# The second block's root ahead of the loop, its solve dealt sooner, and some small products moved, in a delta-rule attention with two MLPs behind it

## The chip, the cores and the metric

One core of a Trainium2 chip runs the whole program. The metric is the device time in microseconds (us) of one execution, as the median of timed runs. The engines are TensorE (PE in the rows; PEld is its loading of weights), VectorE (DVE), ScalarE (ACT), GpSimd (POOL) and SyncE (SP), which issues most DMAs. Each engine works through its instructions in the order in which the program has them and waits where an operand is not ready.

## The reference

Three stages, all in float32. The first is a recurrent attention with a delta rule, for 4 batches of 8 heads, 768 tokens, head size 48:

```
k_n = k / (norm(k) + 1e-6)
for t in range(768):
    y[t]  = q[t] @ state
    v_old = state^T @ k_n[t]
    state = state + beta[t] * outer(k_n[t], v[t] - v_old)
```

The second mixes its output by Fourier transforms over tokens and features, normalizes, and adds an MLP (384 to 1536 to 384). The third is a gated MLP whose gate is a product over tokens (768 x 768). The change touches only the first.

## The kernel before

**Chunks and steps.** The 768 tokens of a head are cut into 12 chunks of 64. The loop runs over 48 chunks (4 batches of 12, numbered `bc`, the batches staggered), each with all 8 heads of its batch. Within a chunk the recurrence is a triangular system of 64 x 64, and its inverse is put together from two 32 x 32 triangles that are inverted on VectorE and a product between them. Eight chunks make a block: block 0 is chunks 0 to 7, and there are 6 blocks.

**What a chunk passes through.** `stage_a(bc)` multiplies keys by keys and by queries on TensorE (16 matmuls as the trace counts them below chunk 24, 8 above) and copies the results to a tile `gak` on ScalarE. `prep(blk)` on VectorE gathers the triangles of 8 chunks and transposes them (L254, L261), and takes their diagonal, the squared norms (L263). `root(blk)` takes their square root on ScalarE (L141) and has GpSimd clear some triangles (L146). `solve(blk)` is the inversion on VectorE: scaling (L153 on), some 30 rounds of multiply and add (L308, L313), and two transposes into the tile `Tc` (L327). For blocks 1 to 4 `prep` of the next block, and then its `root`, stand inside `solve`, ahead of and between these last two transposes; `solve` does not go on to this `prep` while `stage_a` has not been issued for the chunks of the next block. `merge(g8, ...)` joins the two triangles of a pair of chunks by small products (32 each, 64 where it does a first and a second half), `diag` copies from `Tc` on ScalarE, and `stage_b`, `stage_c`, `stage_d` apply the inverse and update the state; `stage_c` ends in a subtraction on VectorE (L495) for which `stage_d` of the same chunk waits.

**The first block.** It is solved ahead of the loop in another form, `halves(0)`: VectorE inverts four 16 x 16 triangles instead of two of 32, and TensorE joins them by small products, `right(q)` (64 matmuls) and `left(q)` (72) for each pair of chunks `q`, each with a copy on ScalarE behind it. `left(q)` needs the copy of `right(q)`. `busy(1, 512)` is two matmuls of 512 columns whose result nobody reads. Keys and queries of chunks 0 to 7 are multiplied by `pairs0`, and for the queries ScalarE copies the result (L583).

**The loop** runs over steps t = -3 to 47. Step t has `stage_d(t)`, `stage_c(t + 1)`, `stage_b(t + 2)`, in odd steps a `merge` for the pair after, and `stage_a` some 20 chunks ahead. A step with t mod 8 = 5 starts a new block: at t = -3 for block 0, and at t = 5 the first merge that uses block 1's `Tc`. The solve of the next block is dealt out between: `Spread(gen, total)` advances `solve` until the sum of the costs that it yields (in ns) has reached a share of `total`, here (i + f) / 8, with i the step within the block and f = 0.5, 0.65 and 1 at three places of a step. Before, steps up to 4 issue one `stage_a` each and step 4 two (chunks 23 and 24), and the root of block 1 stands at the end of step -3.

**What fixes the order.** `chain()` ties each instruction of an engine to the one before it, so each engine's order is the program's. DMAs are issued on SyncE's queue in program order as well, with `load_kq` the keys and queries of a chunk (448 KB), `load_kv` keys and values (192 KB).

Of the kernel before, what the change touches and what calls it, by code (L numbers as in the profile page):

```python
# [23 lines left out]
NBC = B * NC  # L24
BLK = 8
NB = NBC // BLK
# [4 lines left out]
HEAD = 24  # L31
# [13 lines left out]
CF = dict(  # L45
    skew=4, ring=20, kq=5, qt=3, mb=2, cvd=3, cve=2, kn=4, sv="hhhhhd", few=3,
    warm=8, keep=1, last=1, cuts=(0.5, 0.65), dfs=(1, 1, 1, 1, 2, 2, 3, 1, 2, 2, 3, 0), cvt=(0, 0, 0, 1, 2, 2, 1, 1, 0, 0, 0, 0), early=5, first=8, ahead=3,
    turns=(4, 6, 7, 9, 10, 12, 13, 15, 16, 16, 17, 17, 18, 18, 19, 20), stats=(((0, 1, 2, 3, 3), (2,)), ((21, 22, 22), (23, 24, 25))),
)
# [17 lines left out]
class Kernel:  # L67
# [36 lines left out]
    def load(self, out, in_):  # L104
        return self.nc.sync.dma_start(out=out, in_=in_)
# [13 lines left out]
    def attention(self, cp, pg, pe, p, x, filler, after_solves):  # L119
        nc, a, load = self.nc, self.a, self.load  # L120
# [16 lines left out]
        def root(blk):  # L137

            Tf, T, Tw, sq = preps[blk]
            n0 = pe.tile([128, 32], F32, name="n0", bufs=2)  # L140
            nc.scalar.sqrt(n0, sq)  # L141
            if blk:

                for n in (16, 8, 4, 2, 1):
                    t = Tw[:, n : n + 1056].rearrange("p (m q) -> p m q", q=66 * n)[:, :, : 32 * n]
                    nc.gpsimd.memset(t.rearrange("p m (r w) -> p m r w", w=32)[:, :, :, :n], 0.0)  # L146
            preps[blk] = Tf, T, sq, n0
# [33 lines left out]
        def pairs0(n, i):  # L181

            pa = self.bank("pa", [128, 2 * HP, C])
            for g in range(2 * HP):
                k, y = (gas[m][i // 2][:, i % 2 * 2 + g // HP, g % HP] for m in "k" + n)
                for r, q in ROWS:
                    nc.tensor.matmul(pa[q, g], lhsT=k[r], rhs=y[r], start=True, stop=True)
            return pa

        def both0(i, at):  # L190
            return gas[i // 2 * 4, 4][:, i % 2 * 2 : i % 2 * 2 + 2, :, at : at + C].rearrange("p a b c -> p (a b) c")
# [10 lines left out]
        def load_kq(bc):  # L202
            if bc < HEAD:
                if 8 <= bc and bc % 2 == 0:
                    t = pe.tile([112, HP, 4 * C], F32, name="kq", bufs=CF["kq"]).rearrange("p a n -> p (a n)")
                    kqs[bc], kqs[bc + 1] = (t[:, i * HP * 2 * C : (i + 1) * HP * 2 * C].rearrange("p (a n) -> p a n", a=HP) for i in range(2))
                    load(out=t.rearrange("p (c n) -> p c n", c=2), in_=a["kc"][:, bc - 8 : bc - 6])
            elif bc < NBC:
                kqs[bc] = pe.tile([112, HP, 4 * C], F32, name="kq", bufs=CF["kq"])
                load(out=kqs[bc], in_=a["kq"][bc])  # L210

        def stage_a(bc):
            kq = kqs.pop(bc)
            if bc % 4 == 0:
                ring(bc)
            pa = self.bank("pa", [128, HP, 2 * C])
            for hp in range(HP):
                if bc < HEAD:
                    for r, q in ROWS:
                        nc.tensor.matmul(pa[q, hp], lhsT=kq[r, hp, C:], rhs=kq[r, hp], start=True, stop=True)  # L220
                else:
                    nc.tensor.matmul(pa[:, hp], lhsT=kq[:, hp, 2 * C :], rhs=kq[:, hp, : 2 * C], start=True, stop=True)  # L222
            if bc < HEAD:

                copy_g(gas[bc][:, :, C : 2 * C], pa[:, :, C:])
                nc.scalar.copy(out=gas[bc][:, :, :C], in_=pa[:, :, :C])
            else:
                copy_g(gas[bc][:, :, C : 2 * C], pa[:, :, C:])
                nc.vector.tensor_tensor(out=gas[bc][:, :, :C], in0=pa[:, :, :C], in1=mask_a(bc, C).to_broadcast([128, HP, C]), op=MUL)
            if bc < HEAD:  # L230
                if bc % 2 and bc + 2 * CF["kq"] < HEAD:
                    load_kq(bc + 2 * CF["kq"] - 1)
            else:
                load_kq(bc + CF["kq"])
            seen_a[0] = bc + 1
# [301 lines left out]
        for n in "kq":  # L537
            t = p.tile([128, 4, HP, GA], F32, name="gak", bufs=3).rearrange("p a b c -> p (a b c)")[:112, :2048]
# [25 lines left out]
        def busy(n, cols):  # L564
            wb = self.bank("pd", [128, cols])
            for i in range(n):
                nc.tensor.matmul(wb, lhsT=warm[:, :128], rhs=warm[:, :cols], start=True, stop=True)
# [9 lines left out]
                next(first)  # L577
        for _ in first:
            pass
        root(0)  # L580
        right, left = halves(0)
        for i in range(4):
            nc.scalar.copy(out=both0(i, 0), in_=pairs0("q", i))  # L583
        for bc in range(8, 16):
            stage_a(bc)
        busy(CF["last"], 512)
        for part, q in ((right, 0), (right, 1), (left, 0), (left, 1)):
            part(q)
        mask_q(0)
        for _ in prep(1):  # L590
            pass

        self.chain()

# [2 lines left out]
        solver, c1, c2 = None, *CF["cuts"]  # L597
        R = CF["ring"]
        T0 = -3

        lead = {-3: HEAD, -2: HEAD + 1, 0: HEAD + 2, 2: HEAD + 3, 4: HEAD + 4}
        rest = {-3: ((right, 2), (right, 3)), -2: ((left, 2),), -1: ((left, 3),)}
        for t in range(T0, NBC):
            j, i = divmod(t + 11, 8)
            if i == 0 and j < NB:
                if solver:
                    solver.finish()
                solver = Spread(solve(j), 28600 if j < NB - 1 else 27800)
            deal = lambda f: solver.upto((i + f) / 8)

            part = deal if T0 < t and j < NB else (lambda f: None)
            if light(t) and solver:
                solver.finish()
                solver = None

            if 0 <= t + 2 < NBC and (not light(t) or (t + 2) % 8 == 0):
                values(t + 2)
            if t % 2 == 0 and 2 <= t + 2 < HEAD:
                mask_q(t + 2)
            part(c1)  # L620
            if t >= 0:
                stage_d(t)
                if SEQ[t][1] == NC - 1:
                    fill.extend(filler(SEQ[t][0]))
            new = t % 8 == 5 and t + 3 < NBC
            if new:

                merge((t + 3) // 2, True, False)
                load_kv(t + 3)
                load_kv(t + 4)  # L630
                diag((t + 3) // 2)
            if 0 <= t + 1 < NBC:
                stage_c(t + 1)
            if light(t + 1) and t + 3 < NBC and (t + 3) % 8:
                values(t + 3)
            part(c2)
            if t + R <= HEAD:
                stage_a(t + R - 1)
                if t in lead:
                    load_kq(lead[t])  # L640
            if HEAD <= t + R < NBC:
                stage_a(t + R)
            for half, q in rest.get(t, ()):
                half(q)
            odd = t % 2 and (t + 3) // 2 < NBC // 2
            if t == NBC - 12:
                solver.finish()
                loads, tail = after_solves()
            if t % 2 == 0 and t % 8 != 4 and t + 4 < NBC:
                diag((t + 4) // 2)  # L650
            if (odd or light(t + 1)) and 0 <= t + 2 < NBC:
                stage_b(t + 2)
            if odd:
                g = (t + 3) // 2
                merge(g + 1, (g + 1) % 4 > 0, True)
                if (t + 5) % 8 and t + 5 < NBC:
                    load_kv(t + 5)
                    load_kv(t + 6)
            if light(t + 1):

                for _ in range(CF["dfs"][t - (NBC - 12)]):
                    while fill and next(fill[0], 1) == 1:
                        fill.pop(0)
                for _ in range(CF["cvt"][t - (NBC - 12)]):
                    next(tail, None)
            elif not odd and 0 <= t + 2 < NBC:
                stage_b(t + 2)
            if 2 <= t + 4 < NBC:
                load_qt(t + 4)
            if t == T0:  # L670
                root(1)
                part = deal
            part(1)
            self.chain()
            next(loads, None)
            if t >= NBC // 2:
                next(self.words, None)
            self.chain()
# [757 lines left out]
```

## Time and profile before

| | |
|---|---|
| timed runs, median (lowest to highest) | 869.68 us (868.71 to 870.67) |
| the profiled execution | 866.29 us, its span 864.5 us |
| mean granted TensorE clock | 0.978 |
| PE busy | 811.7 us (94%), 10509 matmuls |
| PEld busy | 772.6 us (89%) |
| DVE busy | 606.2 us (70%) |
| ACT busy | 419.8 us (49%) |

The span is the time from the first to the last instruction; the execution's own time is 1.8 us more. TensorE is busy in most of it, so a place where it is idle, or runs at the lower of its two clocks, is looked for. Times in the rows below are us from the start of the span. A matmul of float32 shows as two records, so a product of 32 small matmuls shows as x64. "issue" marks time in which an engine waited for nothing that the profile shows.

### The profile page before, as it was taken

How to read it: one execution, taken by the hardware profiler on the slowest of the kernel's cores; microseconds unless marked ns; L12 is line 12 of the kernel's file. 1: busy time of each engine (PE TensorE's matmuls, PEld its weight loads, DVE VectorE, ACT ScalarE, POOL GpSimd, SP SyncE). 2: the span in 40 equal slices, each digit the busy share in tenths (PEclk: the TensorE clock that was granted, in tenths of full speed). 3: DMA queues.
4: the chain of work that ended last, by engine and by line, in shares of the span. 5: the costliest groups of instructions: out<-in, count | busy, mean ns of one | idle time of the engine just before them, and what ended most of it. 6: DMA issues, size and time to landing. Idle time of an engine off the chain costs nothing.

```text
span 864.5 us, 25181 instructions
## 1 busy us (share of the span) xinstructions
PE 811.7 (94%) x10509; PEld 772.6 (89%) x10509; DVE 606.2 (70%) x1797; ACT 419.8 (49%) x1070; POOL 6.3 (1%) x40
## 2 busy tenths in 40 slices
PE   7696999897888899999999999999999999999998
PEld 7686887786778799989999999999999999899998
DVE  6396999898977898675463793436688378476563
ACT  3476878896756644233223362223471362553632
POOL 0000000000000000000000000000000000000000
PEclk9778999999999999999999999999999999999999
DMA  9344666555461600001022411112101201101101
GB/s 229 112 114 127 168 180 185 166 165 150 129 173 49 235 4 1 2 0 29 1 59 83 134 28 28 29 43 67 46 1 39 72 5 49 59 18 42 52 1 55
DMA packets 57955, 67.63 MB, mean 78 GB/s; under 512 B 31857, under 2 KB 48978, under 8 KB 57842
## 3 DMA queue, kind: packets, MB, share of 16 engines
q1 hardware_dynamic: 57698, 65.89, 26.4%
q8 instruction: 82, 1.34, 0.6%
q14 instruction: 31, 0.25, 0.1%
q10 hardware_dynamic: 144, 0.15, 0.1%
HBM read 53.62 MB, written 4.72 MB: 67 GB/s over the span
## 4 chain that ended last, share of the span: by engine, by line
PE 79%; DVE 9%; ACT 7%; issue 4%; DMA 1%; SPq 0%; ACTq 0%; DVEq 0%
PE bankX L917 17%; PE bankY L930 15%; PE bankX L1115 10%; PE bankX L1095 6%; PE bankX L1063 6%; PE bankY L1143 5%; PE bankY L494 3%; PE bankY L479 2%; PE bankZ L449 2%; PE bankX L222 2%; PE bankV L930 2%; PE bankX L730 2%; PE bankY L514 1%; PE bankY L513 1%; PE bankX L220 1%
## 5 line engine op out<-in xcount | busy, mean ns | idle before, releaser
L930 PE MATMUL bankY<-w,hx 128*128 128x384 f32 x756 | 147.2, 336 | 0.0
L917 PE MATMUL bankX<-uh,w 128*128 128x384 f32 x504 | 137.7, 340 | 0.7 <-DVE ul L839 0.7
L930 PEld LDWEIGHTS bankY<-w,hx 128*128 128x128 f32 x756 | 132.4, 188 | 0.5 <-issue 0.3
L922 DVE SCALAR_TENSOR_TENSOR hx<-bankX,hx 128x384 fp32r<-128x384 f32 x84 | 46.1, 549 | 75.8 <-ACT hx L921 73.3
L921 ACT ACTIVATE hx<-bankX 128x384 fp32r<-128x384 f32 x84 | 41.2, 490 | 112.3 <-PE bankX L917 107.6
L917 PEld LDWEIGHTS bankX<-uh,w 128*128 128x128 f32 x504 | 92.1, 188 | 1.2 <-DVE ul L839 0.9
L1115 PE MATMUL bankX<-w,A 128*128 128x384 f32 x504 | 88.8, 334 | 0.0
L1115 PEld LDWEIGHTS bankX<-w,A 128*128 128x128 f32 x504 | 87.6, 188 | 0.0
L917 PE MATMUL bankX<-ul,w 128*128 128x384 f32 x252 | 85.1, 338 | 0.0
L494 PE MATMUL bankY<-gak,WU 64*64 64x112 f32 x704 | 45.7, 266 | 10.5 <-issue 6.4
L514 PE MATMUL bankY<-WU,gak 64*64 64x48 f32 x768 | 49.5, 222 | 1.4 <-ACT x L531 1.4
L1095 PE MATMUL bankX<-xh,s 128*128 128x384 f32 x192 | 50.0, 338 | 0.0
L313 DVE TENSOR_TENSOR Ts<-Ts,tm 128x108 f32<-128x108 f32 (+10 forms) x216 | 48.8, 261 | 0.9
L308 DVE TENSOR_TENSOR tm<-Ts 128x108 f32<-128x108 f32 (+10 forms) x216 | 48.5, 260 | 0.4
L1104 ACT CAST u<-hx 128x384 fp32r<-128x384 f32 x32 | 15.8, 514 | 66.7 <-DVE hx L1102 66.7
L494 PEld LDWEIGHTS bankY<-gak,WU 64*64 64x64 f32 x704 | 35.9, 137 | 13.1 <-issue 7.4
L917 PEld LDWEIGHTS bankX<-ul,w 128*128 128x128 f32 x252 | 47.3, 188 | 0.0
L479 PE MATMUL bankY<-gak,TT 64*64 64x96 f32 x768 | 45.0, 258 | 1.5 <-ACT n L141 1.3
L514 PE MATMUL bankY<-Sb,cw 48*64 48x48 f32 x704 | 44.9, 220 | 1.4 <-DVE cw L495 1.4
L513 PE MATMUL bankY<-Sb,cw 48*48 48x48 f32 x640 | 37.1, 206 | 9.8 <-DVE cw L495 7.4
L1063 PE MATMUL bankX<-s,xh 128*128 128x512 f32 x144 | 45.9, 395 | 0.0
L513 PE MATMUL bankY<-WU,gak 64*64 64x48 f32 x704 | 43.5, 220 | 0.9 <-issue 0.8
(238 smaller groups left out, 1830.8 us busy)
## 6 DMA issues: line engine op xcount, KB each, us to landing
kq<-in_kq_dram SPq DMA_DIRECT2D x24, 448.0 KB, 4.0
qt<-in_qt_dram SPq DMA_DIRECT2D x48, 196.0 KB, 3.9
gak<-in_kv_dram SPq DMA_DIRECT2D x48, 192.0 KB, 4.1
w<-in_w_dram SPq DMA_DIRECT2D x24, 384.0 KB, 6.5
out_dram<-x SPq DMA_DIRECT2D x24, 192.0 KB, 1.9
kq<-in_kc_dram SPq DMA_DIRECT2D x8, 448.0 KB, 9.8
x<-x SPq DMA_DIRECT2D x96, 36.0 KB, 1.9
s<-in_wi_dram SPq DMA_DIRECT2D x6, 512.0 KB, 4.3
```

Of the source, the lines that this page charges most:

```text
L308: nc.vector.tensor_tensor(out=tm, in0=T[:, r, k : k + 1].to_broadcast(sh), in1=T[:, k : k + 1, :k].to_broadcast(sh), op=MUL)
L313: nc.vector.tensor_add(o, o, tm)
L479: nc.tensor.matmul(pb[h, hp].rearrange("p t d -> p (t d)"), lhsT=tt[h, o + hp], rhs=kv[h, hp], start=True, stop=True)
L494: nc.tensor.matmul(pc[h, hp], lhsT=w[h, hp, :C], rhs=gas[bc][h, hp, : C + D], start=True, stop=True)
L513: nc.tensor.matmul(ps[C * i : C * i + n - C, hp], lhsT=k[:, C:n], rhs=u, start=not last, stop=end)
L514: nc.tensor.matmul(po[hs[1 - i], hp], lhsT=k[:, :C], rhs=u, start=not last, stop=end)
L917: nc.tensor.matmul(ph, lhsT=w1[f][i][:, c * 128 : c * 128 + 128], rhs=cur[k][:, c], start=(c + j == 0), stop=(c == 2 and j == 2))
L922: nc.vector.scalar_tensor_tensor(out=hl, in0=ph, scalar=0.0, in1=hh.bitcast(F32), op0=MAX, op1=SUB)
L930: nc.tensor.matmul(acc[t], lhsT=hx[i][:, t * 128 : t * 128 + 128], rhs=w2[e][k], start=(e == 0 and j == 0), stop=(e == 11 and j == 2),)
L1063: nc.tensor.matmul(pv, lhsT=xT[t][i][:, c, kk * 128 : kk * 128 + 128], rhs=wi[2 * c + 1][k], start=(c + j == 0), stop=(c == 2 and j == 2))
L1095: nc.tensor.matmul(pu, lhsT=wi[2 * c][i][:, f * 128 : f * 128 + 128], rhs=xT[hf][k][:, c], start=(c + j == 0), stop=(c == 2 and j == 2))
L1115: nc.tensor.matmul(acc, lhsT=A[:, m, o, i, kk], rhs=Bo[name, kk][:, k], start=(kk + j == 0), stop=(kk == 2 and j == 2))
```

## The change

Ahead of the loop: three of the four query copies stand ahead of `root(0)`; two more `stage_a` (16, 17) and then a third (18) come in; `busy` goes; `root(1)` comes to the end of this part. In the loop: `stage_a` runs two chunks further ahead up to step 1 (19 in step -3 to 23 in step 1), with none in steps 2 and 3; the loads of chunks 24 to 26 are issued together in step -3, 27 in step -1, 28 in step 1. `right` and `left` of the third pair stand at the end of step -2, `right(3)` at the end of step -1 and `left(3)` at that of step 0. The solve of block 1 is dealt from the beginning of step -3, as if it had a total of 34000 instead of 28600.

```diff
@@ -577,18 +577,21 @@
                 next(first)
         for _ in first:
             pass
+        for i in range(3):
+            nc.scalar.copy(out=both0(i, 0), in_=pairs0("q", i))
         root(0)
         right, left = halves(0)
-        for i in range(4):
-            nc.scalar.copy(out=both0(i, 0), in_=pairs0("q", i))
-        for bc in range(8, 16):
+        nc.scalar.copy(out=both0(3, 0), in_=pairs0("q", 3))
+        for bc in range(8, 18):
             stage_a(bc)
-        busy(CF["last"], 512)
-        for part, q in ((right, 0), (right, 1), (left, 0), (left, 1)):
-            part(q)
+        for half, q in ((right, 0), (right, 1), (left, 0)):
+            half(q)
+        stage_a(18)
+        left(1)
         mask_q(0)
         for _ in prep(1):
             pass
+        root(1)
 
         self.chain()
 
@@ -598,17 +601,15 @@
         R = CF["ring"]
         T0 = -3
 
-        lead = {-3: HEAD, -2: HEAD + 1, 0: HEAD + 2, 2: HEAD + 3, 4: HEAD + 4}
-        rest = {-3: ((right, 2), (right, 3)), -2: ((left, 2),), -1: ((left, 3),)}
+        lead = {-3: (HEAD, HEAD + 1, HEAD + 2), -1: (HEAD + 3,), 1: (HEAD + 4,)}
         for t in range(T0, NBC):
             j, i = divmod(t + 11, 8)
             if i == 0 and j < NB:
                 if solver:
                     solver.finish()
-                solver = Spread(solve(j), 28600 if j < NB - 1 else 27800)
+                solver = Spread(solve(j), 34000 if j == 1 else 28600 if j < NB - 1 else 27800)
             deal = lambda f: solver.upto((i + f) / 8)
-
-            part = deal if T0 < t and j < NB else (lambda f: None)
+            part = deal if j < NB else (lambda f: None)
             if light(t) and solver:
                 solver.finish()
                 solver = None
@@ -634,14 +635,10 @@
             if light(t + 1) and t + 3 < NBC and (t + 3) % 8:
                 values(t + 3)
             part(c2)
-            if t + R <= HEAD:
-                stage_a(t + R - 1)
-                if t in lead:
-                    load_kq(lead[t])
-            if HEAD <= t + R < NBC:
-                stage_a(t + R)
-            for half, q in rest.get(t, ()):
-                half(q)
+            if t + R + 2 < HEAD or HEAD <= t + R < NBC:
+                stage_a(t + R + 2 * (t < 4))
+            for bc in lead.get(t, ()):
+                load_kq(bc)
             odd = t % 2 and (t + 3) // 2 < NBC // 2
             if t == NBC - 12:
                 solver.finish()
@@ -667,9 +664,13 @@
                 stage_b(t + 2)
             if 2 <= t + 4 < NBC:
                 load_qt(t + 4)
-            if t == T0:
-                root(1)
-                part = deal
+            if t == -2:
+                right(2)
+                left(2)
+            if t == -1:
+                right(3)
+            if t == 0:
+                left(3)
             part(1)
             self.chain()
             next(loads, None)
```

## Rows read from the trace of the kernel before

**Rows 1.** The page's part 2: tenths in 40 slices of 21.6 us.
```profile
DVE  6396999898977898675463793436688378476563
...
PEclk9778999999999999999999999999999999999999
```

**Rows 2.** The chain that ended last, 76 to 82 us: start, length, what.
```profile
76.71 1.33 DVE Cc L254 x2
...
78.07 1.91 DVE Ts L261
...
80.19 2.00 DVE Tc L327 x2
```

**Rows 3.** Timeline of PE: opening, step 0, stall at step 5, products at both clocks.
```profile
15.11 2.52 PE L187 MATMUL bankX<-gak 48*64 48x64 f32 x49 [2.29 <-issue]
...
25.35 1.12 PE L567 MATMUL bankY<-TT 128*128 128x512 f32 x2
...
26.41 0.79 PE L393 MATMUL bankY<-Tc,gak 32*32 32x16 f32 x72
...
46.62 1.92 PE L220 MATMUL bankX<-kq 48*64 48x128 f32 x16
...
53.21 0.25 PE L513 MATMUL bankY<-WU,gak 64*64 64x48 f32 x1
...
68.38 0.98 PE L494 MATMUL bankY<-gak,WU 64*64 64x112 f32 x16 [0.56 <-ACT WU L481]
...
69.19 1.04 PE L220 MATMUL bankX<-kq 48*64 48x128 f32 x16
...
82.25 1.06 PE L447 MATMUL bankZ<-Tc,gak 32*32 32x32 f32 x32 [6.14 <-DVE w L153]
...
83.24 1.76 PE L494 MATMUL bankY<-gak,WU 64*64 64x112 f32 x16
```

**Rows 4.** Timeline of DVE: start, length, operation; in brackets idle before, releaser.
```profile
43.98 0.18 DVE L153 TENSOR_SCALAR w<-n 128x32 f32<-128x32 f32 x1 [13.96 <-ACT n L141]
...
66.13 0.60 DVE L495 TENSOR_TENSOR cw<-qt,bankY 112x448 f32<-112x448 f32 x1
...
76.29 0.42 DVE L229 TENSOR_TENSOR gak<-bankX,mk 128x256 f32<-128x256 f32 x1 [5.66 <-ACT gak L196]
```

**Rows 5.** Timeline of DVE in the opening.
```profile
24.99 1.01 DVE L382 STREAM_TRANSPOSE V<-Ts 128x512 f32<-128x512 f32 x1
...
29.83 0.19 DVE L263 COPY sq<-Ts 128x32 f32<-128x32 f32 x1
```

**Rows 6.** The chain that ended last, 36 to 44 us.
```profile
36.90 3.44 issue
...
43.72 0.24 ACT n L141
```

**Rows 7.** The page's parts 3 and 6: the instruction queue; one key load.
```profile
q8 instruction: 82, 1.34, 0.6%
...
kq<-in_kq_dram SPq DMA_DIRECT2D x24, 448.0 KB, 4.0
```

**Rows 8.** Windows: length; busy us (count) of five engines; clock, DMA share, GB/s.
```profile
15.10:22.30 7.20, 7.19 (x125) 7.19 (x127) 7.20 (x60) 3.89 (x13) 0.93 (x3) 0.76 1.01 234
...
30.90:34.90 4.00, 3.29 (x128) 2.81 (x128) 0.00 (x0) 2.24 (x7) 0.00 (x0) 0.72 0.23 56
...
34.90:40.30 5.40, 1.94 (x128) 1.70 (x128) 0.00 (x0) 0.73 (x2) 0.00 (x0) 0.50 0.48 124
...
82.20:88.90 6.70, 6.65 (x136) 5.90 (x136) 4.35 (x18) 2.21 (x7) 0.15 (x1) 0.62 0.39 97
```

**Rows 9.** Timeline of ACT in the opening.
```profile
13.04 0.23 ACT L141 ACTIVATE n<-sq 128x32 f32<-128x32 f32 x1 [7.63 <-DVE sq L263]
...
16.07 0.58 ACT L583 COPY gak<-bankX 128x512 f32<-128x512 f32 x1 [1.84 <-PE bankX L187]
...
31.98 0.27 ACT L404 COPY Tc<-bankY 128x128 f32<-128x128 f32 x1 [2.59 <-PE bankY L403]
```

## The prediction

> **What bounds the kernel now.** I read the page's slices first. VectorE is busy for 7 to 9 tenths of nearly every slice up to 280 us, but for 3 tenths of the second (21.6 to 43.2 us) and 6 of the fourth, and TensorE's granted clock is 7, 7 and 8 tenths in the second to the fourth [rows 1]. So the opening has two holes, and the change lies in the opening.
>
> Next, the chain of waits in the fourth slice. At step 5 the matrix of block 1 (Tc, 8 chunks solved at once) is first used by a merge on TensorE. The chain there is VectorE alone: prep(2) in two adds (L254), its transpose (L261) and the two transposes of Tc (L327), which end at 82.2 [rows 2]. TensorE stood idle for 6.14 us before that merge [rows 3]. VectorE's timeline shows why it was late: after 66.13 it had only tails of solve(1) and two small jobs left, and then sat idle 5.66 us until the evictions of step 4 [rows 4]. In the code this is `while seen_a[0] < 8 * blk + 16`: prep(2) stands inside solve(1), ahead of the transposes, and stage_a(23) comes only in step 4.
>
> The other hole: VectorE waits 13.96 us for the root of block 1 [rows 4]. That root is one ScalarE instruction (L141, 0.23 us), ready from the end of prep(1) at 30.0 [rows 5]; but it is written at the end of step -3, behind a merge that TensorE ends only after a 3.44 us stop, and starts at 43.72 [rows 6].
>
> The stops without a releaser are the last thing to see. TensorE's 10509 + 10509 instructions in 82 packets are 256 a packet, 16 KB each [rows 7]. Between stops the trace counts exactly 128 matmuls with their 128 weight loads: 30.9 to 34.9 and 34.9 to 40.3 are two such stretches, 4.0 and 5.4 us long, with 3.3 and 1.9 us of work in them [rows 8]. So small products are limited by instruction fetch, one packet at a time, and the longer stretch is the one with the busier DMA (0.48 against 0.23). With DMA full, at 1.01, the packet begun at 15.1 lasted TensorE 7.2 us [rows 8].
>
> The Trainium skill, "Runtime: NRT & Kernel Launch", Instruction fetch mechanics, has the same 256-instruction blocks, but calls the cost of crossing one "mostly hidden". By that rule the 2.29 us stop in the query products [rows 3] would not return and the first root would lose 0.4 us rather than 3.5; the forecast below would be nearer 855. The rows here contradict it, and I follow the rows.
>
> **The change, part by part.** Times are of the profiled execution, 866.29 us with its 864.5 us span; the three timed runs have a median of 869.68, so I take differences and subtract them from the median.
>
> *Query copies ahead of the first root: a loss.* Order on ScalarE is program order. The root now starts at 13.04; the copy of the third query product waits for TensorE until 16.07 and takes 0.58 [rows 9], because that product is cut by the 2.29 us fetch stop before 15.11 [rows 3]. TensorE's instructions up to there are unchanged, so the stop stays. The root moves to about 16.6, +3.5 us, and VectorE, which has no idle time from there on, moves with it: Tc of block 0 from 25.0 to 28.5, V from 26.0 to 29.5, the end of prep(1) from 30.0 to 33.5 [rows 5]. Bounds: 0 if the stop falls elsewhere, 3.6 if not. I take 3.5.
>
> *Two more stage_a (16, 17) ahead of the products, the two 512-column warm-up matmuls out.* These matmuls took 1.12 us [rows 3] while TensorE waited for VectorE. The two stage_a cost 1.04 each at full clock and fill the same wait, now 3.5 us longer. Nothing either way.
>
> *Second root ahead of the loop: the gain's source.* It comes behind the copy of left(1). Before, right(0) to that copy ran from 26.41 to 31.98 [rows 3, 9], 5.6 us with two fetch stops in it. Now it starts at 28.5 and carries stage_a(18) too, 1.0 to 1.9 us: 35.5. Bounds: 33.7 (prep(1) ends) to 39 (one more slow fetch). So solve(1) starts at 35.7 rather than 43.98, 8.3 us earlier.
>
> *Solve dealt over 34,000 rather than 28,600, from the start of step -3.* Summing the yields of solve(1) gives 28,100 with prep(2), 22,500 without. Before, VectorE needed 22.15 us from 43.98 to 66.13 [rows 4] for what the plan counts as 5.5/8 of 28,600 = 19.7, two masks and one or two query subtractions, so the plan's units are real time. After, 5.5/8 of 34,000 = 23.4 stand there, 3.7 more: this subtraction comes at 35.7 + 22.2 + 3.7 = 61.6 in place of 66.1. The rest of the solve is 4.7 us: Tc is ready by 66.4, the next subtraction at 67. prep(2) needs stage_a(23), which now lies in step 1, so the 5.66 us idle goes. Root 2 goes into step 3 with it.
>
> *Steps -3 to 0.* By the count of 128 a fetch boundary falls 46 matmuls into right(0), near 28.5. Two more, 3.3 and 4.0 us apart, lead to 35.8, where 18 matmuls of the first merge are left. Before, the stretch from the end of the 3.44 us stop (40.34 [rows 6]) to step 0 (53.21 [rows 3]) took 12.9 us. Now the same stretch has right(2) and right(3) more and left(3) less (64 + 64 - 72 = 56 matmuls, 0.79/72 each [rows 3], 0.6 us), stage_a(19) and the merge's start more (2.2 us at half clock), and left(2) waits for the copy of right(2) (0.7 us): 35.8 + 12.9 + 3.5 = 52.2 for step 0, 1 us earlier than before. Bounds: 49.5 if the clock is full from here; 58 if the three key loads of step -3 (3 x 448 KB [rows 7], ahead of two value loads in SyncE's queue) slow two fetches to the 7.2 us of the full DMA [rows 8].
>
> *Steps 0 to 5.* Before, 53.21 to the merge's arrival at 82.25 - 6.14 = 76.11: 22.9 us. Steps 0 to 4 now have three stage_a fewer (3.1 us) and left(3) more (0.8): 20.6, so arrival at 72.8. VectorE's 67 us for the last subtraction, needed in step 4 about 4 us ahead of the arrival, is just not late. Tc (66.4) is ready. Gain at the merge: 82.25 - 72.8 = 9.4.
>
> *The clock behind the stall.* From 82.2 to 88.9 the granted clock is 0.62 [rows 8]: 5.1 us at half. The L494 products there take 1.76 against 0.98 [rows 3]. Without the stall I take 2.0 of these back (bounds 0 and 2.5).
>
> From step 6 on, the instructions and their order are the same, and the solver starts with TensorE as before, so the 11.4 us should be kept. 869.68 - 11.4 = 858.3; I write 858.
>
> **Rivals.**
> *The opening eats half of it.* The key loads are three in a row, and fetches fall behind them: step 0 at 58, arrival at 78.6, gain 3.6 + 2.0 = 5.6, so 864. For it: the 5.4 us stretch has one such load in it [rows 8]. Against: by then the stages between are long and fetch could hide.
> *Better than that.* The clock comes back by step -2 and fetches hide: step 0 at 49.5, arrival 70.1, gain 12.1 + 2.3: 855. The half clock up to 53 in products with 48 rows (1.92 against 1.04 [rows 3]) and the counts of 128 speak against. The rule of the Trainium skill's page named above, Runtime: NRT & Kernel Launch, that crossings are hidden, would make this the likely case.
> *VectorE's debt, paid at step 13.* It is nearly full after step 5 [rows 1]; if TensorE's lead over it is lost at the next Tc, some 4 us return: 862. Against: solve(2) starts with step 5 in either kernel.
> *Slower: the clock stays at half.* More idle time before step -3 and steps paced by VectorE may keep TensorE at half clock past 53. A step at half costs 0.88 for its stage_a and 0.78 for its L494 products [rows 3], with the other products about 2.8 us. Over five steps that is 14 us less the missing stage_a, 12: arrival at 84.8 and no clock given back, 2.5 us late: 872. It decides from four steps on. Against: before, the clock came back at step 0 after work as thin as this.
> *That it does not do what it says:* root 2 stuck behind left(1)'s copy until 39 or later. Even then Tc is ready at 39.2 + 28.1 + 2.7 = 70, still ahead of the arrival; the time is 858 to 861.
>
> **How the numbers follow.** The forecast has 0.50 (855.5 to 861.5 on its own); better 0.12; opening 0.18; debt at step 13 0.08; slower 0.07; something that cancels it 0.05. The likeliest gives 858. The range 853.5 to 866 takes in the better case, the opening and the debt; outside it stay the last two and some tails. A measurement of this kernel tells 0.2% (1.7 us) from no change. Faster: 0.88; same 0.05; slower 0.07.
>
> **What would show it.** Right: the first L141 near 16.6, the second near 35.5, VectorE busy from there on; L254 of prep(2) ahead of 62; no idle of several us before the first merge of step 5, at about 73; clock 1.0 behind it; 128-matmul stretches still in the opening. Wrong: the first root at 13, so my loss is too large; step 0 at 55 or later; a subtraction on VectorE holding TensorE in steps 2 to 4; half clock past 55; or a new stop at step 13, with the gain at step 5 whole and gone later.

## The result, and the profile after

The changed kernel takes 858.11 us (median of 4 runs, 854.67 to 861.56) against 870.17 us for the kernel before, measured beside it: a ratio of 0.986, 95% interval 0.9816 to 0.9904. Two later comparisons, e1 and e11 below, gave 0.9886 (0.9858 to 0.9913) and 0.987 (0.9848 to 0.9892). By the medians the gain is 12.1, 9.2 and 10.7 us in the three, so 9 to 12 us, while single runs of one kernel lie up to 12 us apart (e3). The two profiled executions are 8.1 us apart, 858.22 with a span of 856.4 us against 866.29.

The page's slices after the change, to be read against [rows 1]:

```profile
DVE  4968998998969997683653892526688377486563
...
PEclk8869999999999999999999999999999999999999
```

VectorE's two holes are filled (9 for 3 in the second slice, 8 for 6 in the fourth), but the third slice has 6 for 9: part of the idle time has moved there. The clock has 9 for 8 in the fourth slice, where the stall was, and 6 for 7 in the third.

TensorE's timeline of the changed kernel, with step 0's first matmul, the first merge of step 5 and the product behind it:

```profile
16.12 2.93 PE L187 MATMUL bankX<-gak 48*64 48x64 f32 x49 [3.63 <-issue]
...
32.54 0.44 PE L403 MATMUL bankY<-Yh,V 32*32 32x16 f32 x31 [1.04 <-issue]
...
49.32 0.41 PE L403 MATMUL bankY<-Yh,V 32*32 32x16 f32 x17 [2.51 <-issue]
...
55.47 0.34 PE L513 MATMUL bankY<-WU,gak 64*64 64x48 f32 x1
...
76.92 0.69 PE L447 MATMUL bankZ<-Tc,gak 32*32 32x32 f32 x32
77.55 0.98 PE L494 MATMUL bankY<-gak,WU 64*64 64x112 f32 x16
```

The merge has no wait in brackets any more and starts at 76.92 instead of 82.25; the product behind it takes 0.98 instead of 1.76 [rows 3]. This is where the gain comes in. Step 0, though, starts at 55.47, 2.3 us later than before (53.21).

The window behind the merge has full clock, and 135 matmuls in 4.2 us where 136 took 6.7 [rows 8]:

```profile
76.90:81.10 4.20, 4.20 (x135) 3.75 (x132) 3.83 (x13) 4.06 (x14) 0.16 (x1) 1.00 0.97 254
```

The two roots on ScalarE (13.04 and 43.72 before [rows 6, 9]):

```profile
17.97 0.23 ACT L141 ACTIVATE n<-sq 128x32 f32<-128x32 f32 x1
...
35.11 0.23 ACT L141 ACTIVATE n<-sq 128x32 f32<-128x32 f32 x1
```

VectorE, as in [rows 4]: solve(1) starts at 35.37 and not 43.98, but then the first subtraction waits.

```profile
35.37 0.35 DVE L153 TENSOR_SCALAR w<-n 128x32 f32<-128x32 f32 x1 [0.42 <-ACT n L141]
...
58.13 0.62 DVE L495 TENSOR_TENSOR cw<-qt,bankY 112x448 f32<-112x448 f32 x1 [6.58 <-PE bankY L494]
...
66.99 1.41 DVE L254 SCALAR_TENSOR_TENSOR Cc<-gak,mk 128x512 f32<-128x512 f32 x2
68.32 0.61 DVE L495 TENSOR_TENSOR cw<-qt,bankY 112x448 f32<-112x448 f32 x1
...
70.93 2.15 DVE L327 STREAM_TRANSPOSE Tc<-Ts 128x512 f32<-128x512 f32 x2
```

The reader is to see the 6.58: at step 0 VectorE is ahead of TensorE by more than 6 us in this execution, so its early start is not what the opening goes by. Tc is ready at 73.1, 3.8 us ahead of the merge.

Whether the gain stays can be read from one ScalarE copy, that of the WU tile, for chunks 7, 15 and 47. First before, then after:

```profile
88.08 0.48 ACT L481 COPY WU<-bankY 128x384 f32<-128x384 f32 x1 [0.51 <-PE bankY L479]
...
128.16 0.48 ACT L481 COPY WU<-bankY 128x384 f32<-128x384 f32 x1 [1.02 <-PE bankY L479]
...
280.84 0.48 ACT L481 COPY WU<-bankY 128x384 f32<-128x384 f32 x1 [0.31 <-PE bankY L479]
```

```profile
80.55 0.49 ACT L481 COPY WU<-bankY 128x384 f32<-128x384 f32 x1
...
119.45 0.48 ACT L481 COPY WU<-bankY 128x384 f32<-128x384 f32 x1
...
272.55 0.48 ACT L481 COPY WU<-bankY 128x384 f32<-128x384 f32 x1 [0.27 <-PE bankY L479]
```

7.5 us ahead at chunk 7, 8.7 at chunk 15, 8.3 at the last: nothing is given back.

### The profile page after: what moved, and what is told of

It reads as the page before. It is cut to its first block, busy times and chain, and to the rows that moved or that the text cites. A ratio compares the mean times of both kernels' runs of the same rounds, so it can differ in the third digit from the quotient of the medians.

```text
span 856.4 us, 25178 instructions
## 1 busy us (share of the span) xinstructions
PE 813.4 (95%) x10507; PEld 775.3 (91%) x10507; DVE 606.2 (71%) x1797; ACT 420.4 (49%) x1070; POOL 6.3 (1%) x40
## 4 chain that ended last, share of the span: by engine, by line
PE 67%; DVE 4%; issue 1%; ACT 1%; ACTq 0%
PE bankX L918 17%; PE bankY L931 15%; PE bankX L1116 10%; PE bankX L1096 6%; PE bankX L1064 6%; PE bankY L1144 5%; PE bankV L931 2%; PE bankX L731 2%; PE bankZ L1144 1%; PE bankX L747 1%; PE bankY L494 0%; PE bankY L514 0%; PE bankY L479 0%; PE bankX L725 0%; DVE cw L495 0%
## 5 line engine op out<-in xcount | busy, mean ns | idle before, releaser
L514 PE MATMUL bankY<-WU,gak 64*64 64x48 f32 x768 | 52.7, 229 | 1.2 <-ACT x L531 1.1
L514 PE MATMUL bankY<-Sb,cw 48*64 48x48 f32 x704 | 47.3, 226 | 3.2 <-issue 1.9
L1105 ACT CAST u<-hx 128x384 fp32r<-128x384 f32 x32 | 15.8, 514 | 66.4 <-DVE hx L1103 66.4
L513 PE MATMUL bankY<-Sb,cw 48*48 48x48 f32 x640 | 39.2, 211 | 7.4 <-DVE cw L495 6.9
L513 PE MATMUL bankY<-WU,gak 64*64 64x48 f32 x704 | 45.9, 228 | 0.1
```

The source lines that it names most:

```text
L513: nc.tensor.matmul(ps[C * i : C * i + n - C, hp], lhsT=k[:, C:n], rhs=u, start=not last, stop=end)
L514: nc.tensor.matmul(po[hs[1 - i], hp], lhsT=k[:, :C], rhs=u, start=not last, stop=end)
```

## The experiments

Theory A: the gain is the wait of prep(2) for stage_a(23), with the low clock behind it, and the other parts of the change move things that do not bound. Rival B: VectorE's earlier start is the gain. Each comparison is with the kernel before on the same chip.

**e1, the changed kernel again.**

> The changed kernel once more, beside the others on one chip. Theory A (the gain is the stall at step 5 and the low clock behind it; the opening lost about 2 us): profile against profile 8 us, so 861 to 862 against 870. Rival B (the gain is 11 to 12 us as forecast, and the profile of before was a quick one): 858 against 870.

857.85 us against 867.05, ratio 0.9886 (0.9858 to 0.9913). In this execution step 0 starts at 52.75 and the first merge of step 5 at 74.30, 2.7 and 2.6 us earlier than in the one above. TensorE's timeline of e1, with the stop in left(2), step 0 and the merge:

```profile
46.60 0.41 PE L403 MATMUL bankY<-Yh,V 32*32 32x16 f32 x17 [1.20 <-issue]
...
52.75 0.34 PE L513 MATMUL bankY<-WU,gak 64*64 64x48 f32 x1
...
74.30 0.69 PE L447 MATMUL bankZ<-Tc,gak 32*32 32x32 f32 x32
```

So one execution's opening is uncertain by nearly 3 us, and neither 8 nor 12 us is excluded.

**e2, stage_a two chunks ahead, alone.** The kernel before, with

```diff
-        for bc in range(8, 16):
+        for bc in range(8, 18):
...
-        for part, q in ((right, 0), (right, 1), (left, 0), (left, 1)):
+        for part, q in ((right, 0), (right, 1), (left, 0)):
             part(q)
+        stage_a(18)
+        left(1)
...
-            if t + R <= HEAD:
-                stage_a(t + R - 1)
-                if t in lead:
-                    load_kq(lead[t])
-            if HEAD <= t + R < NBC:
-                stage_a(t + R)
+            if t + R + 2 < HEAD or HEAD <= t + R < NBC:
+                stage_a(t + R + 2 * (t < 4))
+            if t in lead:
+                load_kq(lead[t])
```

> The kernel before with one part of the change: stage_a runs two chunks further ahead (16, 17, 18 ahead of the loop, 19 to 23 in steps -3 to 1); the second root stays at the end of step -3, the solve at 28600, products and query copies where they were. Theory A (the stall at step 5 was the wait of prep(2) for stage_a(23)): solve(1) starts at 44 as before, but Tc is ready about 44 + 28 + 3 = 75, the first merge of step 5 is at 76 to 77, and the time 7 to 8 us below before. Rival B (VectorE's late start at 44 made the stall): the merge waits till 80 or later, the gain is at most 2 us.

858.95 us, ratio 0.9899 (0.9874 to 0.9924): 8.1 us below before, of the 9.2 of e1 on the same chip, so nearly the whole gain. VectorE and TensorE of e2:

```profile
44.93 0.18 DVE L153 TENSOR_SCALAR w<-n 128x32 f32<-128x32 f32 x1 [15.05 <-ACT n L141]
...
75.28 2.16 DVE L327 STREAM_TRANSPOSE Tc<-Ts 128x512 f32<-128x512 f32 x2
```

```profile
77.50 0.69 PE L447 MATMUL bankZ<-Tc,gak 32*32 32x32 f32 x32 [0.63 <-DVE Tc L327]
```

VectorE waits 15 us for the root, longer than before, and still the merge waits only 0.63 us. The early root is not needed for the gain.

**e3, the root ahead, without stage_a.** The changed kernel with stage_a and the key loads in their old steps.

> The changed kernel with stage_a and the key loads back in the old steps (chunks 8 to 15 ahead of the loop, 23 and 24 in step 4): root 2 ahead of the loop, the solve over 34000, moved products and query copies stay. Theory A: VectorE starts near 35 but waits for the evictions of step 4 as before; 6 us of VectorE work (prep(2), Tc) still follow them, so TensorE idles 5 to 6 us at step 5, and the gain is 0 to 2 us. Rival B: the stall is gone, gain 7 us or more.

864.73 us, ratio 0.9968 (0.9941 to 0.9995): 2.3 us below before. VectorE and TensorE of e3:

```profile
33.54 0.26 DVE L153 TENSOR_SCALAR w<-n 128x32 f32<-128x32 f32 x1 [0.29 <-ACT n L141]
...
73.64 0.42 DVE L229 TENSOR_TENSOR gak<-bankX,mk 128x256 f32<-128x256 f32 x1 [5.67 <-ACT gak L196]
```

```profile
79.59 1.06 PE L447 MATMUL bankZ<-Tc,gak 32*32 32x32 f32 x32 [6.15 <-DVE w L153]
```

VectorE starts 10.4 us earlier than before, idles the same 5.67 us for step 4's evictions, and TensorE stands the same 6.15 us, to a hundredth of [rows 3, 4]. With e2 this decides between A and B: B falls. (TensorE came to the merge 2.7 us earlier than before, 73.44 for 76.11. That this is about the 2.3 us between the medians says little: the profiled execution, 860.19, is the fastest of e3's twelve.)

**e4, the first root ahead of the query copies again.** `root(0)` moved up above the loop of three copies.

> The changed kernel with the first root ahead of the query copies again, as before. Theory A (VectorE's start sets the opening): the first root is back at 13 to 14 instead of 18, right(0) starts 3 to 4 us earlier, step 0 at 52 to 53 instead of 55.5, and the time is 2 to 3 us below the changed kernel. Rival C (instruction fetch and the half clock set TensorE's pace up to step 0; VectorE sat idle 6.6 us there anyway): within 0.7 us of the changed kernel.

856.85 us, ratio 0.9877 (0.9845 to 0.991), not to be told from e1. I had put the earlier step 0 under A and the null result under a rival C; the run bears out C. The first root is at 12.78, and yet step 0 starts where it did in e1:

```profile
52.92 0.25 PE L513 MATMUL bankY<-WU,gak 64*64 64x48 f32 x1
```

**e5, key loads spread.**

```diff
-        lead = {-3: (HEAD, HEAD + 1, HEAD + 2), -1: (HEAD + 3,), 1: (HEAD + 4,)}
+        lead = {-3: (HEAD,), -2: (HEAD + 1,), 0: (HEAD + 2,), 2: (HEAD + 3,), 4: (HEAD + 4,)}
```

> The changed kernel with the key loads of chunks 24 to 28 issued as before, one each in steps -3, -2, 0, 2 and 4, and not three in step -3. Theory A: the stop of 1.4 to 2.5 us in the middle of left(2) is a packet of instructions that stands behind 1.3 MB of keys and 0.8 MB of values; it shrinks to under 1 us, step 0 comes 1 to 2 us sooner (51 to 52 against 52.8 to 55.5), and the time falls by 1 us or so, at the edge of what the rounds tell. Rival: the packet is late for the value loads alone; no change of the stop.

859.24 us, ratio 0.9887 (0.9858 to 0.9917). The stop in left(2) is gone and step 0 starts at 50.55, 2.2 us ahead of e1, a little more than the 1 to 2 expected. The stop in left(2) is 1.2 to 3.2 us in the six executions that have the three loads together and the products in this order (2.51 in the first, 1.20, 1.47, 3.17, 1.75 and 1.38 in e1, e4, e7, e8 and e11). The DMA queue shows it too: the instruction packet that lands 1.4 to 1.6 us before the stop ends starts at 46.69 in the first execution and at 43.77 in e1, and the same packet of e5 at 41.21. But the time did not fall: a stop of 3.16 us came at step 1, in front of an L513 matmul at 58.56, and the merge of step 5 is at 74.91 (e1: 74.30). A stop near there is not new, though: e4, e8 and e11 have one of 1.3 to 1.6 us at 59.8 to 59.9, beside that in left(2). TensorE's timeline of e5:

```profile
44.46 1.05 PE L403 MATMUL bankY<-Yh,V 32*32 32x16 f32 x64 [0.24 <-ACT Yh L394]
...
58.56 0.20 PE L513 MATMUL bankY<-WU,gak 64*64 64x48 f32 x1 [3.16 <-issue]
```

**e6, products back.** right(2), right(3) in step -3, left(2) in -2, left(3) in -1.

> The changed kernel with right(2) and right(3) back in step -3, left(2) in step -2 and left(3) in step -1. Theory A (TensorE up to step 0 goes at the pace of packets of 128 matmuls, whatever their order): step 0 within 1 us later, for 16 matmuls more ahead of it, the stall at step 5 stays away, the time within 1 us of the changed kernel. Rival (the move spreads the small products and saves stops): step 0 is 3 us later or more, and so is the end.

856.72 us, ratio 0.9869 (0.985 to 0.9889); step 0 at 52.63, within 1 us of e1's as theory A had it. By itself the move is worth nothing that shows.

**e7, matmuls to fill the stops.**

```diff
+            fb = self.bank("pd", [128, 256])
+            for i in range(n):
+                nc.tensor.matmul(fb, lhsT=self.idn, rhs=mk[:, :256], start=True, stop=True)
```

> The changed kernel with six matmuls of 256 columns whose result nobody reads, two each behind right(1), left(1) and right(2) (12 records, 0.3 us each at full clock, so 3.4 us of TensorE in all, 6.8 at half). Theory A (between packets TensorE has time to spare): the issue stops shrink by what is put in, and step 0 is at most 1 us later; if the work keeps the clock up, the half clock from 32.6 to 56.5 ends earlier and step 0 comes up to 3 us sooner. Rival (TensorE's own work is the bound): 3 to 5 us later.

859.15 us, ratio 0.9891 (0.987 to 0.9912). This run parts clock from fetch, up to the end of left(2). The first fence has a window of e1, the second one of e7 (columns as in [rows 8]; the clock is the third from last):

```profile
32.60:52.70 20.10, 17.55 (x509) 15.43 (x500) 16.02 (x86) 10.88 (x36) 0.84 (x6) 0.50 0.55 145
```

```profile
32.60:48.50 15.90, 11.18 (x391) 9.03 (x383) 15.09 (x74) 8.65 (x28) 0.83 (x6) 0.99 0.57 152
...
48.50:52.00 3.50, 3.50 (x76) 3.28 (x76) 2.72 (x13) 2.21 (x9) 0.00 (x0) 0.54 0.28 90
```

The granted clock is 0.99 instead of 0.50 over 16 us, and step 0 starts at 53.04, 0.3 us after e1's. TensorE did its work there in 11.2 of 15.9 us (2.3 us of it the four matmuls put in behind left(1) and right(2)) and waited for the rest, 3.17 us of it in left(2):

```profile
47.78 0.43 PE L403 MATMUL bankY<-Yh,V 32*32 32x16 f32 x28 [3.17 <-issue]
```

So up to left(2) the half clock is not what the opening goes by: work done twice as fast only makes the stops longer, and the last of them, 3.17 us, is longer than all that the matmuls put in took in this window. Behind left(2) the run shows nothing on it: there the clock was at half in e7 too (0.54), with TensorE busy for all of the 3.50 us.

**e8, the solve over 28600.**

> The changed kernel with the solve of block 1 dealt over 28600 like the others. Theory A: VectorE idles 5 us at step 0, so the pace of dealing is no bound there; prep(2) falls into step 3 and Tc is ready 3 to 5 us later, near 75, with the first merge of step 5 at 74 to 77: within 1.5 us of the changed kernel. Rival (34000 is needed): TensorE idles 3 us or more at step 5 again.

857.69 us, ratio 0.9881 (0.9859 to 0.9903). The last two transposes of Tc start at 75.22, the merge waits 1.19 us for them and starts at 77.42, just outside the 74 to 77 expected. So this pace is a bound in that execution, but one so small that it does not show in the time.

**e9, one packet less.** The kernel of e5 without right(2) and left(2).

> The kernel of e5 (key loads spread) without right(2) and left(2): the join of the two halves of block 0's third pair of chunks is left out, so that pair's inverse is not the reference's. 136 matmul records, a little over one packet, are gone ahead of step 0. Theory A (TensorE goes at the pace of packets there, 3.5 to 5 us each): step 0 at 46 to 47 instead of 50.6, 3.5 us or more sooner. Rival (their own work and the copy between them): 64 + 72 records take 1.1 + 1.5 us and 0.3 of waiting at the clock of the changed kernel, 2.9 at half and 1.9 at full clock; step 0 at 48 to 49.

854.75 us, ratio 0.9843 (0.9808 to 0.9879). Step 0 starts at 47.32, 3.2 us before e5's, between the two expectations; with openings that scatter by nearly 3 us this decides nothing.

**e10 and e12, the three undone together; e11, the changed kernel beside e12.** Root first, loads spread and products back: the edits of e4, e5 and e6 in one kernel.

> The changed kernel with the first root ahead of the query copies, the key loads spread and the products back in their old steps; what stays of the change is stage_a two chunks ahead, root 2 ahead of the loop and the solve over 34000. Theory A: each of the three was worth nothing that can be measured, so 856 to 859, the same as the changed kernel. Rival (they add up): 2 us or more below it, 855 or less against 867 to 870.

853.05 us against 867.32, ratio 0.9845 (0.9808 to 0.9881). That was lower than expected, so I ran both once more on one chip.

> The changed kernel, on the same chip as e12. Theory A (query copies, key loads and product places are worth nothing together): within 1.5 us of e12. Rival (e10 was better by what it undid): 3 us or more above e12.

> The kernel of e10 once more, on the same chip as e11. Theory A: within 1.5 us of e11, near 856 to 858 against 867 to 870. Rival: 3 us or more below e11, near 853, and its opening (the first merge of step 5 at 73) again earlier than the changed kernel's (74 to 77).

857.05 us for the changed kernel and 852.47 for the combined, ratios 0.987 (0.9848 to 0.9892) and 0.9831 (0.9808 to 0.9854). Theory A falls on this point: the three, of which none showed by itself, are worth 4.6 us together on this chip. The two intervals still overlap by 0.06%, but each of the five runs of the combined kernel (851.65 to 854.68) is below each of the four of the changed one (854.96 to 857.37). (Beside e10 the changed kernel did not run, so e10 has only its ratio to before.) The combined kernel is the fastest one here that computes everything. In its opening the merge of step 5 starts at 73.54 (72.95 in e10), against 75.01 for e11:

```profile
73.54 0.69 PE L447 MATMUL bankZ<-Tc,gak 32*32 32x32 f32 x32
```

That accounts for 1.5 us. The two profiled executions are 2.5 us apart (854.96 and 852.47), so 1.0 us comes later, in steps whose order of work is the same in both. From the WU copy of chunk 7 to that of chunk 47, first in e11, then in e12 (columns as in [rows 8]):

```profile
78.61:269.75 191.14, 170.35 (x5220) 152.45 (x5211) 170.55 (x624) 143.88 (x427) 2.47 (x18) 0.97 0.55 154
```

```profile
77.18:267.27 190.09, 168.21 (x5220) 150.48 (x5208) 170.55 (x624) 144.18 (x426) 2.48 (x18) 0.98 0.55 155
```

The work is the same and TensorE is busy 2.1 us less for it, at a granted clock of 0.98 for 0.97. The mean clock of all runs differs likewise: 0.982 to 0.986 in the five of e12, 0.974 to 0.978 in the four of e11. So at least part of the 4.6 us goes with the clock. What raises it, and which of the three undone parts it needs, stays open.

## Why the prediction was right, and where it was not

**The stall at step 5: right, and its cause right.** It was read from the chain and the 5.66 us of idle [rows 2, 4]: prep(2) waited for stage_a(23). e2 and e3 show it from both sides: with stage_a ahead the stall goes, without it the stall stays.

**"Second root ahead of the loop: the gain's source": wrong.** This is the step that failed. The second root came at 35.11, where 35.5 was forecast, and VectorE started at 35.37 for 35.7. But e3 has that start and keeps the stall; e2 has neither and loses it. The forecast carried the 8.3 us through the solve to an earlier Tc, and took the earlier stage_a as a mere condition. It was the other way round: stage_a(23) was the last wait, and with it in time a solve that starts at 44.93 ends at 77.4 (e2), 0.6 us behind TensorE. The sum survived this, because its 9.4 us is counted to TensorE's arrival: Tc came at 73.1 where 66.4 was forecast, and was still in time.

**"Query copies ahead of the first root: a loss": the move was right, the cost was not.** The root went from 13.04 to 17.97, with a fetch stop of 3.63 us ahead of the product; VectorE's norms were 0.9 us late in this execution too (13.92 for 13.00), so I count 4.0 for 3.5. In the nine profiled executions with this order the root lies between 15.80 and 17.97. e4 undid it and nothing came of it, because VectorE was not the bound: it sat idle 6.58 us at step 0, waiting for TensorE's product. The subtraction forecast for 61.6 came at 68.32 for that wait. One side sum was off: without the 2.29 us stop the root would lose 3.6 - 2.29 = 1.3 us by the same rows, and not 0.4.

**Steps -3 to 0: the size was off by 3.3 us in that execution.** 52.2 was forecast, 55.47 measured (52.75 and 53.38 in e1 and e11). The three key loads do hold a packet of instructions back, as the rival said: the 2.51 us in left(2) goes with e5. It is a smaller price than the rival's 58, and in e5 a longer stop at step 1 took its place. The 58 had no row for its price: in the window of 7.2 us TensorE is busy for 7.19 [rows 8], so that stretch is full of work and shows no slow fetch. Three signs that the prediction named for being wrong, or right, went against it here: step 0 was later than 55, the half clock lasted past 55 (0.50 from 50.0 to 56.5, with TensorE busy all the time), and prep(2)'s L254 came at 66.99 and not ahead of 62.

**Fetch against clock: right to follow the rows.** Stops came back in all profiles, up to 3.6 us each, and e7 shows that the half clock cost nothing up to left(2). The Trainium skill's "mostly hidden" (Runtime: NRT & Kernel Launch, Instruction fetch mechanics) does not hold for such products here.

**Steps 0 to 5 and the clock: right.** 20.6 us forecast, 21.45 measured (55.47 to 76.92). The clock behind the stall gave back 2.5 us by the two windows (6.7 and 4.2 us) for 2.0 forecast.

In sum, the merge came 5.3 us earlier for 9.4 forecast, and the profile pair shows 8.1 us for 11.4. The median fell by 12.1. Forecast and median agree to 0.1 us (858 and 858.11), and that is luck: the fall was 9.2 and 10.7 us in the two later comparisons, and the sum held one wrong attribution and one loss that cost nothing.

## What to carry to other kernels

When two conditions stand ahead of a stalled step, ask which is met last, and undo the parts of the change one by one: here stage_a two chunks ahead carried 8.1 of 9.2 us by itself (e2 beside e1), and all the rest without it, with the visible hole in VectorE's timeline filled, 2.3 (e3). Long idle time of an engine is no gain in itself while another sets the pace. And where stops without a releaser come every 128 float32 matmuls, count instructions, not busy time: up to left(2) neither a faster clock (e7) nor an earlier operand (e4) helped here.

## What the hardware showed that was not expected

- With six matmuls of 256 columns put in between, the granted clock in the opening was 0.99 instead of 0.50 for 16 us (e7), at no gain in time.
- A stop for instructions that is taken away can come back one or two packets later: 2.51 us in left(2) at 49.3, only 0.24 there in e5 (for a ScalarE copy), 3.16 us at 58.6.
- Runs of one kernel spread over 9 us in the 17 of the kernel before (863.51 to 872.68) and over 12 in the 12 of e3, so single effects under 3 us were not resolved. The slower runs of a kernel mostly have the lower granted clock: e5's fastest run, 853.23 us, has 0.986 and its slowest, 861.46 us, 0.972. In the profiles the dips lie in steps of the same work too: from 140 to 160 us the clock is 0.77 in e7 and 1.00 in e5, and from chunk 15's WU copy to chunk 31's e7 took 83.0 us and e5 75.5.
